# Moving the mixer's first product in front of a couple's scores in a fused attention and MLP kernel

## The chip, the cores and the metric

The kernel runs on one core of a Trainium2 chip. The time is the device time of one execution in microseconds (us). Of the kernel before, three timed runs gave 573.91, 575.65 and 576.12 us, so the median is 575.65 us. One more execution was taken with the hardware profiler: its own time is 570.46 us, and the span from its first to its last instruction is 568.7 us.

The core has five engines with a queue each: TensorE (PE, the matrix products; its weight loads are shown apart as PEld), VectorE (DVE), ScalarE (ACT), GpSimd (POOL) and SyncE (SP, which here only issues DMAs). Each engine works through its own queue in order. An instruction that needs another engine's result waits on a semaphore, and everything behind it in its queue waits with it.

## The reference

The reference is attention with normalised queries and keys, and then a mixing layer and an MLP on its output. There are 8 batches, 12 heads, 448 tokens and 64 values per head:

```python
q_n, k_n = rmsnorm(q, g_q), rmsnorm(k, g_k)
scores = q_n @ k_n.transpose(0, 1, 3, 2) / sqrt(64)
attn = softmax(scores)
x = (attn @ v).transpose(0, 2, 1, 3).reshape(8, 448, 768)
h = x.transpose(0, 2, 1) @ U @ V            # U: 448 x 32, V: 32 x 448, over the tokens
u = x + h.transpose(0, 2, 1)
out = u + relu(u @ w_ch1) @ w_ch2           # 768 -> 3072 -> 768
```

## The kernel before

The heads are worked on in groups of four, three groups to a batch, numbered gi = 0 to 23. A group has two couples of two heads, written (batch, pr) with pr = 0 to 5; couple (2, 0) is the first of group 6.

**Staging of a group.** Queries and keys are loaded (`load`, issued by SP), squared and summed (`squares`, `sums`), and scaled by their root mean squares (`scale_all`; from group 6 on by POOL, lines 198 and 202). From group 6 on the turning of queries and keys, so that the 64 head dimensions lie on the partitions, is done by DMA: `turn_dma` (lines 388 to 394) issues four DMA transposes on SP's queue, in the order qT of the first couple, kT of the first, qT of the second, kT of the second. Then `take_dma` (line 399) multiplies each couple's qT by the gains on POOL, in place. A couple's scores need that product and the couple's kT.

**A couple's scores.** `Spair` (line 445) makes one couple's scores. Two products go into two small PSUM tiles `sl` (line 455, 64 rows of the array, 448 columns), four into two large tiles `sc` (line 464), and one last block, whose keys are the remaining 64 of both heads together, into a third small tile (`Slast`, lines 473 to 480, product at line 476). Each is followed by its exponential on ACT (lines 457, 468, 477). For a couple that comes with the remaining rows of the group before (`rest`), the last block is a step of its own; for the others it is issued inside `Spair` (line 466).

**Values.** `Vall` (line 551) multiplies the exponentials by the values and divides by the sums (DVE, lines 545 and 546). `Rest` (line 597) does the last 64 rows of a group of four heads (PE line 568, DVE lines 580 and 584, output `xr`).

**The mixer and the MLP of a batch.** `mix_t` (line 604) is the mixer's first product: 16 narrow products with U (line 609, 32 columns of the array each, 12 on `x` and 4 on `xr`), copied to `tT` by DVE (line 613). `mix_two` (line 617) is the second: products with V into two `sc` tiles (line 626), four additions on DVE (line 633), and DMA transposes of the result into `uT` (line 639, SP). `up` (line 689) is the first MLP product, 1.14 by the planner's cost, with a ReLU on ACT. `down` (line 733) is a quarter of a second MLP product: six products of 384 columns (line 740), cost 0.98; after the fourth quarter DVE adds the residual (line 750) and SP issues the output's DMAs (line 758).

PSUM is a pool `ps` of four small tiles (for `sl`, `po`, `pu`, `ph`, `pv`, `pr`) and a pool `ps_sc` of two large ones (for the `sc` tiles of scores and of `mix_two`).

**What sets the order.** After a front written out by hand, a loop at the end of the function (lines 1051 to 1089) merges two lists as the program is built. `att` holds the attention's steps, `mlp` the pieces of mixer and MLP, each in its own order. `done_at` says how far `att` must be before a batch's pieces may run. `due` says how much attention work should have been issued for the MLP work issued so far; a step of `att` is taken if it is due and `ready` says that the engines' planned clocks (`at`, advanced by `runs`) allow it. Two conditions of `ready` matter here: a couple's scores aren't taken directly behind a piece of the mixer, and not where ACT or DVE are planned to be behind PE. Neither the landing of a DMA nor POOL's work is in `at`.

Of the kernel before, what the change touches and what calls it, by code (L numbers as in the profile page):

```python
# [21 lines left out]
REST = 8.0  # L22
SECOND = 53.0
APART = 3


@with_exitstack
def kernel(
# [322 lines left out]
    at = {"pe": 0.0, "act": 0.0, "dve": 0.0}  # L351
    exp_done = {}

    def runs(eng, us):
        at[eng] = us + (at["pe"] if eng == "pe" else max(at["pe"], at[eng]))
# [86 lines left out]
        runs("act", 0.9 if n == 2 else 0.52)  # L442
        exp_done[(b, pr)] = at["act"]

    def Spair(b, pr, rest=None):
        qT, kT = qk[divmod(b * NPAIR + pr, 2)]
        E = es[(b, pr)] = ep.tile([P, NB, S], BF16, name="E", tag="E")
        ts = [ps.tile([P, 512], FP32, name="sl", tag="ps")[:, :S] for _ in range(2)]
        if rest is not None:
            rest_tile(rest)  # L450
            rest_products(rest)
            rest_norms(rest)
        for i in range(2):
            d = slice(i * D, (i + 1) * D)
            nc.tensor.matmul(ts[i], kT[d, 2 * P:3 * P], qT[d], start=True, stop=True)  # L455
        for i in range(2):
            nc.scalar.activation(E[:, 4 + i, :], ts[i], AF.Exp, scale=scal, bias=bias)  # L457
        runs("pe", 0.4)
        runs("act", 1.04)
        tiles = [ps_sc.tile([P, 2, 512], FP32, name="sc", tag="sc") for _ in range(2)]  # L460
        for r in range(2):
            for i in range(2):
                d = slice(i * D, (i + 1) * D)
                nc.tensor.matmul(tiles[r][:, i, :S], kT[d, r * P:(r + 1) * P], qT[d], start=True, stop=True)  # L464
        if rest is None:
            Slast(b, pr)
        for r in range(2):
            nc.scalar.activation(E[:, 2 * r:2 * r + 2, :], tiles[r][:, :, :S], AF.Exp, scale=scal, bias=bias)  # L468
        runs("pe", 0.4)
        runs("act", 1.78)  # L470
        exp_done[(b, pr)] = at["act"]

    def Slast(b, pr):
        qT, kT = qk[divmod(b * NPAIR + pr, 2)]
        last = ps.tile([P, 512], FP32, name="sl", tag="ps")[:, :S]
        nc.tensor.matmul(last, kT[:, SM:], qT, start=True, stop=True)  # L476
        nc.scalar.activation(es[(b, pr)][:, 2 * NJ, :], last, AF.Exp, scale=scal, bias=bias)  # L477
        runs("pe", 0.2)
        runs("act", 0.52)
        exp_done[(b, pr)] = at["act"]  # L480
# [78 lines left out]
    def rest_products(gi):  # L559
        b = groups[gi][0]  # L560
        va, vl = normed[gi][2:]
        pv = rest_tiles[gi]
        q0 = 0 if b % 2 else SM
        for lp in range(2):
            E = es[divmod(2 * gi + lp, NPAIR)]
            for j in (NJ, *range(NJ)):
                for e in range(2):
                    nc.tensor.matmul(  # L568
                        pv[e * R:(e + 1) * R, lp, :],
                        E[:, 2 * j + (e if j < NJ else 0), q0:q0 + R],  # L570
                        va[:, (lp + 2 * e) * NJ + j, :] if j < NJ else vl[:, lp, e * D1:(e + 1) * D1],
                        start=(j == NJ), stop=(j == NJ - 1))
        runs("pe", 0.36)

    def rest_norms(gi):
        b, h0, _ = groups[gi]
        pv = rest_tiles.pop(gi)
        lo, hi = (0, R) if b % 2 else (R, P)
        r = headp.tile([P, 2], FP32, name="r", tag="r")
        nc.vector.reciprocal(r, pv[:, :, D])  # L580
        for e in range(2):
            rows = slice(e * R, (e + 1) * R)
            c = (h0 + 2 * e) * D
            nc.vector.tensor_tensor(
                x_rest[b % 2][lo:hi, c:c + 2 * D].rearrange("p (h d) -> p h d", d=D),
                pv[rows, :, :D],
                r[rows].rearrange("p h -> p h ()").to_broadcast([R, 2, D]), ALU.mult)
        runs("dve", 0.6)
# [5 lines left out]
    def rest_tile(gi):  # L594
        rest_tiles[gi] = ps.tile([P, 2, D1], FP32, name="pr", tag="ps")
# [166 lines left out]
    att = []  # L762

    def add_att(cost, f, *a):
        att.append((cost, f, a))
# [3 lines left out]
    def weights(n):  # L769
        for f, a in todo[:n]:  # L770
            f(*a)
        del todo[:n]
# [8 lines left out]
    for i, (b, pr) in enumerate(pairs):  # L781
        if b == 0:
            continue
        gi, a = divmod(i, 2)
# [3 lines left out]

        rest = gi - 1 if a == 0 and (pr > 0 or b > APART) else None
        if a == 0 and pr == 0 and b > 1:  # L790
            add_att(0.8, Vall, *pairs[i - 1])
            if gi == DMA_FROM:
                add_att(0.0, sums, gi + 1, 0)
                add_att(0.0, sums, gi + 1, 1)
                add_att(0.0, scale_all, gi + 1)
            if b <= APART:
                add_att(0.5, Rest, gi - 1)
# [63 lines left out]
    done_at = {0: 0}  # L861
# [7 lines left out]
    mlp = []  # L869
# [135 lines left out]
    ia = im = 0  # L1005
    ca = cm = 0.0
# [12 lines left out]
    def due(c):  # L1019

        if c < m_one:
            return min(a_one - 0.01, a_one * c / (m_one - 3.0))
        c -= m_one
        if c < REST:
            return a_one - 0.01
        if c < SECOND:
            return a_one + (a_two - a_one) * (c - REST) / (SECOND - REST)
        return a_two + (a_all - a_two) * (c - SECOND) / (m_end - m_one - SECOND)

    def mixes(f):  # L1030
        return f in (mix_t, mix_two)

    def ready(f, a):
        if f is Spair:
            if im > 0 and mixes(mlp[im - 1][1]):
                return False
            return at["dve"] <= at["pe"] + 0.3 and at["act"] <= at["pe"] + 0.6
        if f is Slast:
            return not after_pair
        if f in (Vall, Rest) and ca >= a_one and (after_pair or after_v):  # L1040
            return False
        if f is sums and a[0] > DMA_FROM:
            return not any(m[1] is mix_t for m in mlp[max(0, im - 1):im + 3])
        if ca >= a_one:
            return True
        if f is Vall:
            return exp_done[a[:2]] <= at["pe"] + 0.1
        return f is not Srows or at["act"] <= at["pe"] + 0.6 and (len(a) == 1 or a[1] is None or at["dve"] <= at["pe"] + 0.9)

    later, turning, mixed, after_pair, after_v = [], False, False, False, False  # L1050
    while ia < len(att) or im < len(mlp):
        if not turning:
            held = []
            for f, a in later:
                if a[0] == DMA_FROM + 2 and not mixed:
                    held.append((f, a))
                else:
                    f(*a)
            later[:] = held
        may_mlp = im < len(mlp) and ia >= done_at[mlp[im][3]]  # L1060
        take_att = ia < len(att) and (not may_mlp or ca <= due(cm) and ready(*att[ia][1:]))
        if take_att:
            c, f, a = att[ia]
            if f is load:
                later.append((f, a))
            else:
                f(*a)
            after_pair = after_pair or f is Spair
            after_v = after_v or f is Vall
            if ia >= a_from:  # L1070
                ca += c
            ia += 1
            if f is scale_all and a[0] < DMA_FROM:
                weights(2)
            if f is T and a == (DMA_FROM - 1, 1):
                nc.vector.memset(kp[:, 2 * NJ:], 0.0)
        else:
            f = mlp[im][1]
            if after_pair and mixes(f) or f is mix_two and max(at["act"], at["dve"]) > at["pe"]:
                e = next((i for i in range(im, len(mlp)) if mlp[i][1] is down), None)  # L1080
                if e is not None and mlp[e][3] < mlp[im][3]:
                    mlp.insert(im, mlp.pop(e))
            after_pair = after_v = False
            c, f, a, _ = mlp[im]
            f(*a)
            turning = f is mix_t or turning and not (f is mix_two and a[1][1] == NW - 1)
            cm += c
            mixed = mixed or f is mix_two and a[1][1] == NW - 1
            im += 1
# [30 lines left out]
```

## Time and profile before

| | |
|---|---|
| median of three timed runs | 575.65 us |
| the profiled execution's own time | 570.46 us |
| its span | 568.7 us |
| PE busy | 561.5 us, 99% of the span |
| ACT busy | 308.5 us, 54% |
| POOL busy | 204.5 us, 36% |
| DVE busy | 189.4 us, 33% |
| products of line 693 (`up`) | 223.9 us, 352 ns each |
| products of line 740 (`down`) | 223.5 us, 326 ns each |

In rows of the profile's timeline the first number is the start in us from the span's start and the second how long the group lasts; then engine, line, operation, output<-inputs, shapes, and the count of merged instructions. In brackets stands how long the engine was idle before and what ended that. A matmul's own duration is longer than the distance to the next one, because products overlap in the array. SPq rows are SP's DMA issues, not the transfers.

### The profile page before, as it was taken

The page shows a single profiled execution, that of the slowest core. Times are in us where ns is not written, and L with a number is a line of the kernel's source. Part 1 is how long each engine was busy: PE and PEld are TensorE (multiplying, and loading weights), DVE is VectorE, ACT ScalarE, POOL GpSimd, SP SyncE. Part 2 cuts the span into 40 slices and gives each one's busy share as a digit, 9 for nine tenths or more (in the row PEclk, how much of TensorE's full clock was granted, in tenths as well). Part 3 has the DMA queues.
Part 4 walks back from the last instruction along what each step waited for, and adds up shares of the span by engine and source line. Part 5 has one row for each costly group of instructions (what it writes and reads, how often), then busy time and mean ns, then how long its engine had stood idle before and what let it go on. Part 6 is the DMA issues. An engine that isn't in the chain of part 4 may idle for free.

```text
span 568.7 us, 11567 instructions
## 1 busy us (share of the span) xinstructions
PE 561.5 (99%) x4756; PEld 321.9 (57%) x4756; DVE 189.4 (33%) x425; ACT 308.5 (54%) x518; POOL 204.5 (36%) x308
## 2 busy tenths in 40 slices
PE   8899999999999999999999999999999999999997
PEld 7665555555555555555556555565465555555555
DVE  6955564312443222521235231532034210410011
ACT  6967760888454776287553677367752544014300
POOL 6874784355332724343522532351531000000000
PEclk9999999999999999999999999999999999999999
DMA  9999999784247633595335735375215200320022
GB/s 241 223 242 240 247 228 179 159 225 114 62 91 171 170 98 63 90 233 144 74 96 107 203 90 125 67 204 128 36 33 86 56 23 0 77 56 0 1 57 56
DMA packets 104830, 68.20 MB, mean 120 GB/s; under 512 B 66633, under 2 KB 100937, under 8 KB 104777
## 3 DMA queue, kind: packets, MB, share of 16 engines
q1 hardware_dynamic: 95124, 57.83, 44.2%
q0 software_dynamic: 9408, 9.44, 10.0%
q8 instruction: 37, 0.61, 0.5%
q10 hardware_dynamic: 244, 0.20, 0.1%
q14 instruction: 17, 0.13, 0.1%
HBM read 52.20 MB, written 11.01 MB: 111 GB/s over the span
## 4 chain that ended last, share of the span: by engine, by line
PE 94%; ACT 4%; DMA 1%; DVE 0%; POOL 0%; issue 0%; POOLq 0%
PE po L740 38%; PE ph L693 37%; PE pv L541 4%; ACT E L435 3%; PE sc L464 2%; PE sl L455 2%; PE sl L476 2%; PE pr L568 1%; PE po L727 1%; PE pv L537 1%; PE sc L430 1%; PE sc L711 1%; PE sc L626 1%; PE pu L609 1%; DMA ob<-in_g_k_dram 1%; PE pt L368 1%
## 5 line engine op out<-in xcount | busy, mean ns | idle before, releaser
L693 PE MATMUL ph<-uT,w1b 128*128 128x448 bf16 x1128 | 223.9, 352 | 0.0
L740 PE MATMUL po<-w2b,hT 128*128 128x384 bf16 x1296 | 223.5, 326 | 0.0
L740 PEld LDWEIGHTS <-hT 128*128 128x128 bf16 x1296 | 122.8, 98 | 84.1 <-issue 7.0
L693 PEld LDWEIGHTS <-w1b 128*128 128x128 bf16 x1128 | 108.2, 98 | 97.6 <-issue 2.2
L700 ACT ACTIVATE hT<-ph 128x448 bf16<-128x448 f32 x187 | 99.7, 550 | 106.9 <-PE ph L693 106.5
L399 POOL TENSOR_SCALAR qT<-qT,gg 128x448 bf16<-128x448 bf16 x36 | 50.4, 1402 | 92.4 <-DMA qT<-qn 77.3
L457 ACT ACTIVATE E<-sl,gg 128x448 bf16<-128x448 f32 x72 | 41.6, 630 | 76.2 <-PE sl L455 75.3
L198 POOL TENSOR_TENSOR qn<-qf,rs 128x384 bf16<-128x384 f32 x36 | 29.9, 830 | 111.9 <-ACT rs L175 106.1
L468 ACT ACTIVATE E<-sc,gg 128x896 bf16<-128x896 f32 x72 | 68.9, 1019 | 0.0
L750 DVE TENSOR_TENSOR ob<-po,x 128x384 f32<-128x384 f32 x46 | 25.6, 557 | 103.7 <-PE po L740 103.0
L167 DVE TENSOR_REDUCE ssq<-sq 128x14 f32<-128x896 f32 x45 | 47.0, 1078 | 23.9 <-ACT sq L141 23.2
L545 DVE RECIPROCAL r<-pv 128x6 f32<-128x6 f32 x42 | 8.2, 195 | 125.4 <-PE pv L541 125.1
L435 ACT ACTIVATE E<-sc,gg 128x896 bf16<-128x896 f32 (+1 forms) x42 | 37.0, 951 | 1.1 <-PE sc L430 0.7
L541 PE MATMUL pv<-va,E 128*128 128x65 bf16 x756 | 35.4, 194 | 0.0
L541 PEld LDWEIGHTS <-E 128*128 128x128 bf16 x756 | 32.4, 98 | 3.2
L198 POOL TENSOR_TENSOR kp<-kf,rs 128x384 bf16<-128x384 f32 x36 | 29.8, 828 | 0.0
L537 PE MATMUL pv<-vl,E 128*128 128x130 bf16 x126 | 27.6, 219 | 0.0
L633 DVE TENSOR_TENSOR x<-sc,x 128x384 bf16<-128x384 f32 x42 | 20.8, 550 | 17.4 <-PE sc L626 17.4
L546 DVE TENSOR_TENSOR x<-pv,r 128x384 bf16<-128x384 f32 x42 | 23.4, 557 | 1.4
L174 ACT ACTIVATE rs<-ssq,eps 128x28 f32<-128x28 f32 x20 | 6.3, 315 | 32.1 <-DVE ssq L167 32.1
L477 ACT ACTIVATE E<-sl,gg 128x448 bf16<-128x448 f32 x36 | 23.3, 646 | 0.0
L206 POOL CAST va<-vf 128x768 bf16<-128x768 f32 x24 | 20.7, 862 | 0.2 <-DMA vf<-in_v_dram 0.2
(130 smaller groups left out, 426.4 us busy)
## 6 DMA issues: line engine op xcount, KB each, us to landing
qf<-in_q_dram SPq DMA_DIRECT2D x23, 448.0 KB, 3.7
kf<-in_k_dram SPq DMA_DIRECT2D x23, 448.0 KB, 4.9
vf<-in_v_dram SPq DMA_DIRECT2D x48, 192.0 KB, 5.5
out_dram<-ob SPq DMA_DIRECT2D x48, 192.0 KB, 2.7
w2b<-in_moe_w_ch_dram POOLq DMA_DIRECT2D x8, 576.0 KB, 15.3
w1b<-in_moe_w_ch_dram POOLq DMA_DIRECT2D x2, 1152.0 KB, 17.6
vf<-in_v_dram SPq DMA_DIRECT2D x48, 32.0 KB, 5.1
w1b<-in_moe_w_ch_dram POOLq DMA_DIRECT2D x1, 1536.0 KB, 28.5
```

Of the source, the lines that this page charges most:

```text
L167: nc.vector.tensor_reduce(ssqs[gi][:, i, :], sqs.pop((gi, i)), AX, ALU.add)
L198: nc.gpsimd.tensor_tensor(main.rearrange("p (t i) d -> p i t d", i=2), src[:, c, :2 * NJ].rearrange("p (i t) d -> p i t d", i=2), rs[:, c, ...
L399: nc.gpsimd.tensor_scalar(qT[:, a], qT[:, a], gg[:, 0:1], None, ALU.mult)
L435: nc.scalar.activation(es[(b, pr)][:, 2 * r:2 * r + n, :], sc[:, :n, :S], AF.Exp, scale=scal, bias=bias)
L457: nc.scalar.activation(E[:, 4 + i, :], ts[i], AF.Exp, scale=scal, bias=bias)
L468: nc.scalar.activation(E[:, 2 * r:2 * r + 2, :], tiles[r][:, :, :S], AF.Exp, scale=scal, bias=bias)
L537: nc.tensor.matmul(pv[:, i].rearrange("p e d -> p (e d)"), E[:, 2 * NJ, w:w + P], vl[:, lp, :], start=True, stop=False)
L541: nc.tensor.matmul(pv[:, i, e, :], E[:, 2 * j + e, w:w + P], va[:, (lp + 2 * e) * NJ + j, :], start=False, stop=(e == 1 and j == NJ - 1))
L693: nc.tensor.matmul(ph, w1b[:, dt, ht * P:(ht + 1) * P], uT[:, dt, off:off + S], start=(dt == 0), stop=(dt == KD - 1))
L700: nc.scalar.activation(hT[:, ht, off:off + S], ph, AF.Relu)
L740: nc.tensor.matmul(po, hT[:, ht, col:col + P], w2b[:, ht, half * HALF:(half + 1) * HALF], start=(ht == 0), stop=(ht == KH - 1))
L750: nc.vector.tensor_tensor(ob[:, h], po, urows(b, col, half), ALU.add)
```

## The change

In the merging loop, ahead of the usual choice, the planner looks whether `mix_t` is among the next four pieces of `mlp` (`NEAR`), and whether the next step of `att` is a `Spair` without `rest` that is due within 1.0 (`AHEAD_OF`), with ACT's and DVE's planned clocks not behind PE's. If so, it issues `mix_t` at once, directly behind it the couple's `Spair` without its last block, and puts the last block (`Slast`) into `att` as the next step, which may be taken after one more piece of MLP.

```diff
+NEAR, AHEAD_OF = 4, 1.0
...
-    def Spair(b, pr, rest=None):
+    def Spair(b, pr, rest=None, late=False):
...
-        if rest is None:
+        if rest is None and not late:
             Slast(b, pr)
...
+        near = next((m for m in range(im, min(im + NEAR, len(mlp))) if mlp[m][1] is mix_t), None)
+        if near is not None and ia >= done_at[mlp[near][3]] and ia < len(att) and not after_pair and not after_v:
+            c, f, a = att[ia]
+            if f is Spair and a[2] is None and ca <= due(cm) + AHEAD_OF and at["act"] <= at["pe"] + 0.6 and at["dve"] <= at["pe"] + 0.3:
+                m = mlp.pop(near)
+                m[1](*m[2])
+                cm += m[0]
+                turning = True
+                f(*a, True)
+                att.insert(ia + 1, (0.0, Slast, a[:2]))
+                for d in done_at:
+                    if done_at[d] > ia:
+                        done_at[d] += 1
+                after_pair = True
+                ca += c
+                ia += 1
+                continue
         may_mlp = im < len(mlp) and ia >= done_at[mlp[im][3]]
```

In the program that is built, this holds at two places. The order of the queues of SP and POOL stays as it was; PE's, ACT's and DVE's differ at these places alone.

First place (couple (2, 0), mixer of batch 1; n down stands for n pieces of `down`):

```text
before: mix_t(1), 3 down, mix_two, 4 down, mix_two, 2 down, Spair(2,0)+Slast, 2 down, turn_dma(7), 1 down, Spair(2,1), 1 down, Vall(2,0)
after:  mix_t(1), Spair(2,0), 3 down, mix_two, 4 down, mix_two, 4 down, Slast(2,0), turn_dma(7), Spair(2,1), 2 down, Vall(2,0)
```

Second place (couple (3, 0), mixer of batch 2):

```text
before: Rest(8), 2 down, Spair(3,0)+Slast, 1 down, mix_t(2), 2 down, mix_two, 1 down, turn_dma(10)
after:  Rest(8), 1 down, mix_t(2), Spair(3,0), 4 down, mix_two, 1 down, Slast(3,0), turn_dma(10)
```

## The prediction

> **What bounds the kernel now.** I read the page first: the busy shares and the chain that ended last.
>
> ```profile
> span 568.7 us, 11567 instructions
> PE 561.5 (99%) x4756; PEld 321.9 (57%) x4756; DVE 189.4 (33%) x425; ACT 308.5 (54%) x518; POOL 204.5 (36%) x308
> ...
> PE 94%; ACT 4%; DMA 1%; DVE 0%; POOL 0%; issue 0%; POOLq 0%
> ```
>
> PE is busy for 99% of the span and carries 94% of the chain. So there are no gaps of PE to fill: a reordering of the same products can gain only what PE loses between unlike products, and any wait that it gives PE is paid in full, since nothing later on PE has idle time into which the delay could vanish. The question is whether the moved products find their inputs ready. I therefore went through the timeline of the first place, from the issue of group 6's DMA transposes to couple (2, 1):
>
> ```profile
> 82.36 1.33 SPq L391 DMA_TRANSPOSE qT<-qn  x1
> 84.22 1.21 SPq L393 DMA_TRANSPOSE kT<-kp  x1
> ...
> 88.17 0.43 PE L609 MATMUL pu<-x,Ub 128*32 128x192 bf16 x12
> ...
> 88.62 3.10 PE L740 MATMUL po<-w2b,hT 128*128 128x384 bf16 x18
> ...
> 91.65 0.34 PE L626 MATMUL sc<-tT,Vr 32*128 32x192 bf16 x8
> ...
> 92.42 1.41 POOL L399 TENSOR_SCALAR qT<-qT,gg 128x448 bf16<-128x448 bf16 x1 [8.45 <-DMA qT<-qn]
> ...
> 94.11 1.40 POOL L399 TENSOR_SCALAR qT<-qT,gg 128x448 bf16<-128x448 bf16 x1 [0.28 <-DMA qT<-qn]
> ...
> 98.27 0.36 PE L455 MATMUL sl<-qT,kT 64*128 64x448 bf16 x2
> ...
> 98.66 1.16 ACT L457 ACTIVATE E<-sl,gg 128x448 bf16<-128x448 f32 x2 [12.36 <-PE sl L455]
> ...
> 98.94 0.36 PE L476 MATMUL sl<-qT,kT 128*128 128x448 bf16 x1
> ...
> 99.14 3.09 PE L740 MATMUL po<-w2b,hT 128*128 128x384 bf16 x18
> ...
> 99.71 0.64 ACT L477 ACTIVATE E<-sl,gg 128x448 bf16<-128x448 f32 x1
> ...
> 100.23 1.92 ACT L468 ACTIVATE E<-sc,gg 128x896 bf16<-128x896 f32 x2
> ```
>
> `mix_t(1)` starts at 88.17, its last product is followed by `down` at 88.62, and couple (2, 0)'s scores begin at 98.27, nearly 10 us later. Between the two POOL multiplies the couple's qT by the gains: it had been idle for 8.45 us until the transpose landed, starts at 92.42 and ends at 93.83. The second row of line 399 is couple (2, 1)'s. In the kernel before the scores come 4.4 us after that product, so its lateness costs nothing. Why it is late is seen in the DMA view of the stretch 82.3 to 88.5, and in the view by tile of qT:
>
> ```profile
> q0 software_dynamic: 1301, 0.98, 103.8%
> ...
> qT<-qn SPq DMA_TRANSPOSE x2, 8.5
> kT<-kp SPq DMA_TRANSPOSE x2, 9.3
> ```
>
> ```profile
> DMA to landing us min/median/max: 2.5/2.5/8.5
> ```
>
> The transposes share the DMA engines with the software queue, on which POOL's issues of w2 are still running; here a transpose takes 8.5 to 9.3 us to land, against 2.5 us in the median of the whole span. kT of the couple, issued at 84.22, lands at about 84.22 + 9.3 = 93.5.
>
> **The change, part by part.** No product, exponential, addition or DMA is added or removed. Two `Spair` go earlier and two last blocks later; neither they nor `mix_t` issue a DMA or anything on POOL, so SP's and POOL's queues keep their order.
>
> First place, the score products. After the change they stand directly behind `mix_t`, so PE reaches them at 88.62, where `down` began before. They need qT, multiplied at 92.42 + 1.41 = 93.83, and kT at 93.5. From a product's end to ACT's start it is 0.03 us here (98.27 + 0.36 against 98.66); with as much for POOL to PE, the scores start at 93.86 and PE waits 93.86 - 88.62 = 5.2 us. Nothing covers this: PE's queue is in order, and the three `down` that stood there wait behind the scores, with them the additions of line 750, the output's DMAs, `mix_two` and, on SP, the transposes into `uT`, all about as much later. Lower bound of the wait: were the first qT to land after 8.5 us, like the one of that row, POOL would end at 82.36 + 8.5 + 1.41 = 92.3, which leaves 3.7 us. Upper bound: were the second multiplication needed too, 94.11 + 1.40 - 88.62 = 6.9 us. I take 5.2, since the built program has the first score product wait for the first multiplication alone.
>
> First place, changes of the kind of product. A `down` quarter is six products; 18 of them take 99.14 to 102.16, where the next scores begin, and 12 take 96.21 to 98.27:
>
> ```profile
> 96.21 2.12 PE L740 MATMUL po<-w2b,hT 128*128 128x384 bf16 x12
> ...
> 102.16 0.36 PE L455 MATMUL sl<-qT,kT 64*128 64x448 bf16 x2
> ```
>
> With two lengths the pace and the loss at the change come out: (3.02 - 2.06) / 6 = 0.16 us a product, and 2.06 - 12 x 0.16 = 0.14, about 0.1 us. Entering or leaving a narrow product costs that. `mix_t` directly in front of the scores saves one such change, and the last block fills the whole array like `down` and costs none beside it: 0.1 us saved at each place, 0.2 in all.
>
> First place, the last block. It now stands directly in front of couple (2, 1)'s scores. That couple's own last block reuses the small PSUM tile that the exponential of line 477 frees. From the rows, a last block's exponential is done 0.39 + 0.64 = 1.03 us after its product starts, and couple (2, 1)'s last block comes 0.20 (98.94 to 99.14) + 0.67 (98.27 to 98.94) + 0.1 = 0.97 us after it: a wait of 0.1 us, between 0 and 0.6 if ACT has something else to end. ACT's order otherwise only lets the two large exponentials go ahead of the last block's. `mix_two` now takes the large PSUM tiles from those: they are done 0.39 + 1.05 (98.66 to 99.71) + 1.92 = 3.4 us after the scores start, and PE needs 0.67 + 0.1 + 18 x 0.16 = 3.7 us to get there. No wait, but if ACT were over 0.3 us late there would be one.
>
> Second place. Here `mix_t(2)` goes ahead of one `down` less behind `Rest(8)`:
>
> ```profile
> 138.04 1.40 POOL L399 TENSOR_SCALAR qT<-qT,gg 128x448 bf16<-128x448 bf16 x1 [1.16 <-DMA qT<-qn]
> ...
> 150.51 2.12 PE L740 MATMUL po<-w2b,hT 128*128 128x384 bf16 x12
> ...
> 150.83 0.59 DVE L584 TENSOR_TENSOR xr<-pr,r 64x128 bf16<-64x128 f32 x2
> ...
> 152.57 0.36 PE L455 MATMUL sl<-qT,kT 64*128 64x448 bf16 x2
> ```
>
> qT is multiplied by 139.4, some 12 us ahead. `mix_t` would start at 150.51 + 6 x 0.16 + 0.1 = 151.6 and needs `xr` for its last products; DVE ends it at 150.83 + 0.59 = 151.42. So nothing is paid, at most 0.2 us if DVE slips; ACT has four `down` for its exponentials, one more than at the first place. That leaves the 0.1 us saved.
>
> PE's clock. A PE idle for 5.2 us may come back at half its rate. This trace shows both sides of it, in the timeline's first row and in stretches (length, then busy time and count by engine, then the granted clock):
>
> ```profile
> 1.36 5.73 PE L245 MATMUL busy<-ident 128*128 128x128 bf16 x72 [1.36 <-POOL ident masks.py:199]
> ```
>
> ```profile
> 0.00:4.60 4.60, 3.24 (x31) 3.25 (x32) 1.04 (x13) 1.53 (x2) 0.86 (x7) 1.00 0.59 184
> ...
> 565.30:567.80 2.50, 0.00 (x0) 0.00 (x0) 0.28 (x1) 0.00 (x0) 0.00 (x0) 1.00 0.30 79
> 567.80:568.70 0.90, 0.00 (x0) 0.00 (x0) 0.00 (x0) 0.00 (x0) 0.00 (x0) 0.51 0.00 0
> ```
>
> At the start, 31 products take 3.24 us, 105 ns each, and the other 41 of the 72 end at 7.09, some 60 ns each: PE begins at about half rate for 3.2 us of work, which costs 31 x 45 ns = 1.4 us. At the end, 2.5 us without a product are followed by a granted clock of 0.51. So I expect a 5.2 us wait to lower the clock, and I price the return like the start: 1.4 us, with ends of 0 (the clock stays) and 3.2 (two such stretches at half rate, 6.5 us of which half is lost).
>
> The Trainium skill, "TensorE: Matmul & The Clock Gate", Part 1, says that the clock halves after an idle window of about 3.4 us, that these windows run freely, and that a busy window restores it. By that, a 5.2 us wait would hold a whole window in (5.2 - 3.4) / 3.4, about half of all phases, and the sum would lack the 1.4 us in the other half. The end of this trace, where 2.5 us sufficed, speaks for the clock to fall more often than that.
>
> **The sum.** 5.2 + 0.1 - 0.2 + 1.4 = 6.5 us. Against the profiled execution that is 570.46 + 6.5 = 577.0 us, and a span of 575.2. The timed runs lie higher, with their median at 575.65; I put the 6.5 us on it: 582.2 us.
>
> **The rivals.**
>
> The wait without the loss of clock: 5.2 + 0.1 - 0.2 = 5.1 us, so 580.8 us. For it: no stretch inside this span shows PE idle for so long, so the fall is inferred from its two ends. Against it: the row at 567.80.
>
> The wait is hidden (the other side). If the software queue has drained a few us earlier in timed runs than in the profiled one, the transposes land after the usual 2.5 us: qT at 84.9, multiplied by 86.3, kT at 86.7, all before PE's 88.62. Then only the saved changes remain: 575.65 - 0.1 = 575.5 us, no measurable difference. It decides at a landing of qT by 88.62 - 1.41 = 87.2, 5.2 us earlier than in this trace; and kT too must land by 88.6 instead of 93.5. Against it: the queue's 103.8% and landings of 8.5 and 9.3 us, which no part of the change touches.
>
> The change pays by more than the 0.2 us: no row shows PE time that it could recover, with PE busy for 99% of the span; it would take 2.9 us.
>
> **How the numbers follow.** This kernel's measurement tells apart about 0.5%, 2.9 us. Wait with loss of clock 0.62, wait alone 0.26, hidden 0.10, a gain 0.02. Both waits are slower by more than 0.5%: slower 0.88, same 0.10, faster 0.02. The low end is the shortest wait without loss of clock, 575.65 + 3.7 - 0.2 = 579.2, less 0.7 for the scatter of the runs: 578.5. The high end is 5.2 + 0.6 - 0.2 + 3.2 = 8.8, so 584.5, and 0.5 for the scatter: 585.
>
> **What would show it.** In the changed profile, a single gap on PE of about 5 us in front of the first products of line 455, at 88.6, ended by POOL's qT of line 399; behind it products of line 740 at twice their pace's time for some 3 us and a granted clock under 1; everything later by 5 to 7 us; at the second place no wait. I am wrong if those products start before 91 us, if qT's landing has moved, or if PE has new gaps elsewhere.

## The result, and the profile after

The changed kernel took 579.86 us (median of six runs, 579.10 to 582.61) against 574.83 us for the kernel before in the same session (572.50 to 576.12). The ratio is estimated at 1.0119, with a 95% interval of 1.0090 to 1.0148: slower, by more than the 0.5% that this measurement tells apart. The plain quotient of the two medians is smaller, 1.0088, just below that interval; the stretches and the second measurement below show which of the two is nearer. The profiled execution took 582.61 us, with a span of 580.8 us.

From the changed kernel's page: the span, the busy times, the granted clock in 40 slices (tenths) and the chain that ended last.

```profile
span 580.8 us, 11566 instructions
...
PE 566.2 (97%) x4756; PEld 324.2 (56%) x4756; DVE 189.9 (33%) x425; ACT 309.4 (53%) x518; POOL 204.5 (35%) x308
...
PEclk9799998999999999999999999999999999999999
...
PE 87%; DMA 4%; POOL 4%; ACT 2%; issue 2%; DVE 0%; SPq 0%; POOLq 0%
```

The products are as many as before (4756). PE's share of the chain fell from 94 to 87%, and DMA and POOL now hold 4% each. The granted clock (PEclk) has two dips, in the second slice and in the seventh (87 to 102 us).

The timeline of SP, PE and POOL at the first place, after the change. Line numbers of the code below the change are one higher than before: `Rest` is line 569, `mix_t` 610, a couple's first scores 456, `down` 741, POOL's gain on qT 400.

```profile
87.51 1.34 SPq L392 DMA_TRANSPOSE qT<-qn  x1
...
89.92 0.22 PE L569 MATMUL pr<-vl,E 128*64 128x65 bf16 x2
...
93.33 0.43 PE L610 MATMUL pu<-x,Ub 128*32 128x192 bf16 x12
...
96.83 1.41 POOL L400 TENSOR_SCALAR qT<-qT,gg 128x448 bf16<-128x448 bf16 x1 [7.71 <-DMA qT<-qn]
...
98.29 0.56 PE L456 MATMUL sl<-qT,kT 64*128 64x448 bf16 x2 [4.45 <-POOL qT L400]
98.63 0.97 PE L465 MATMUL sc<-qT,kT 64*128 64x448 bf16 x4
99.53 5.09 PE L741 MATMUL po<-w2b,hT 128*128 128x384 bf16 x18
104.55 0.34 PE L627 MATMUL sc<-tT,Vr 32*128 32x192 bf16 x8
```

PE is idle for 4.45 us in front of the scores, and the multiplication of qT ends that. kT is hardly sooner: the load of it as PE's weights waits for its transpose until 98.28. Then the 18 products of the next three `down` take 99.53 to 104.55, 5.02 us, where they took 3.03 us before (88.62 to 91.65). The same stretch in windows (length, then busy time and count by engine, PE first, then the granted clock, the DMA share and GB/s):

```profile
93.60:96.79 3.19, 0.24 (x12) 0.01 (x4) 0.36 (x1) 0.00 (x0) 0.00 (x0) 1.00 1.41 134
96.79:98.29 1.50, 0.00 (x0) 0.01 (x1) 0.00 (x0) 0.00 (x0) 1.41 (x1) 0.50 1.39 149
98.29:103.61 5.32, 5.32 (x19) 2.24 (x20) 0.02 (x1) 2.96 (x4) 5.10 (x8) 0.50 0.09 31
103.61:107.00 3.39, 3.39 (x28) 1.85 (x27) 2.48 (x5) 0.00 (x0) 1.75 (x5) 1.00 0.25 61
```

The clock falls to half during the wait and stays there for 5.3 us of work behind it: 19 products in 5.32 us, then, at the full clock, 28 in 3.39 us.

**Where the 12 us between the two profiled spans come from.** Three starts, each of a `Rest`, cut the span into parts that hold the same work in both kernels. In the kernel before:

```profile
84.77 0.22 PE L568 MATMUL pr<-vl,E 128*64 128x65 bf16 x2
...
150.14 0.22 PE L568 MATMUL pr<-vl,E 128*64 128x65 bf16 x2
...
167.87 0.22 PE L568 MATMUL pr<-vl,E 128*64 128x65 bf16 x2
```

and after, beside the row at 89.92:

```profile
162.36 0.22 PE L569 MATMUL pr<-vl,E 128*64 128x65 bf16 x2
...
179.99 0.22 PE L569 MATMUL pr<-vl,E 128*64 128x65 bf16 x2
```

| part | before, us | after, us | difference |
|---|---|---|---|
| start to Rest(5), ahead of any changed instruction | 84.8 | 89.9 | +5.1 |
| Rest(5) to Rest(8), with the first place | 65.4 | 72.4 | +7.1 |
| Rest(8) to the next, with the second place | 17.73 | 17.63 | -0.1 |
| from there to the end | 400.8 | 400.8 | 0.0 |

The first part isn't the change's: the instructions up to there are the same. In this execution PE waited in the front for data and its clock fell there too:

```profile
22.12 0.55 PE L431 MATMUL sc<-qT,kT 64*128 64x448 bf16 x2 [2.47 <-DVE kT L384]
```

```profile
21.69:28.52 6.83, 6.00 (x53) 3.78 (x54) 5.82 (x22) 4.63 (x8) 5.32 (x9) 0.50 0.85 155
```

The wait and half of these 6.0 us of work make 5.5 us, about the difference. The front varies so in both kernels: of the eleven profiles in the table below, three start Rest(5) after 88 us, one of them with the order of the kernel before, and each of the three has a clock of one half for 6.83 us in the front; the other eight start it at 84.7 to 86.0 us and have no such dip. From Rest(5) to the end, which leaves it out, the kernel before takes 568.7 - 84.8 = 483.9 us and the changed one 580.8 - 89.9 = 490.9 us: +7.0 us, or 1.2% of the span. I use this stretch for the experiments.

### The profile page after: what moved, and what is told of

Its sections match the earlier page's. It is cut to its first block, busy times and chain, and to the rows that moved or that the text cites. A ratio compares the mean times of both kernels' runs of the same rounds, so it can differ in the third digit from the quotient of the medians.

```text
span 580.8 us, 11566 instructions
## 1 busy us (share of the span) xinstructions
PE 566.2 (97%) x4756; PEld 324.2 (56%) x4756; DVE 189.9 (33%) x425; ACT 309.4 (53%) x518; POOL 204.5 (35%) x308
## 4 chain that ended last, share of the span: by engine, by line
PE 87%; DMA 4%; POOL 4%; ACT 2%; issue 2%; DVE 0%; SPq 0%; POOLq 0%
PE po L741 36%; PE ph L694 35%; PE pv L542 4%; DMA kf<-in_k_dram 3%; PE sc L465 2%; PE sl L456 2%; DMA qT<-qn 2%; PE sl L477 2%; ACT E L436 1%; POOL sq L145 1%; PE po L728 1%; PE pr L569 1%; PE pv L538 1%; PE sc L712 1%; PE sc L627 1%
```

## The experiments

My theory: all of the loss is at the first place, as a wait for group 6's operands and as work at half clock behind it; the second place gains a tenth of a microsecond. The rivals are in the expectations: that the moves themselves cost something, that the slow products have another cause than the wait, that the operands are late for another reason than the loads of w2.

| kernel | Rest(5) starts | span | Rest(5) to end | PE's wait in front of couple (2, 0) | median | ratio to before, 95% interval |
|---|---|---|---|---|---|---|
| before | 84.77 | 568.7 | 483.9 | - | | |
| changed | 89.92 | 580.8 | 490.9 | 4.45 | 579.86 | 1.0119 (1.0090 to 1.0148) |
| changed, again | 88.79 | 580.2 | 491.4 | 5.12 | 579.30 | 1.0119 (1.0084 to 1.0154) |
| second place only | 84.90 | 568.7 | 483.8 | - | 571.90 | 1.0002 (0.9985 to 1.0018) |
| first place only | 85.06 | 577.0 | 491.9 | 5.62 | 578.47 | 1.0110 (1.0086 to 1.0134) |
| wait filled | 84.69 | 574.0 | 489.3 | 1.33 beside the filling | 576.00 | 1.0076 (1.0058 to 1.0094) |
| last block inside | 85.69 | 575.7 | 490.0 | 4.69 | 578.84 | 1.0129 (1.0104 to 1.0155) |
| no last w2 | 84.91 | 568.7 | 483.8 | none | 571.27 | 1.0000 (0.9980 to 1.0019) |
| before, no last w2 | 88.57 | 572.8 | 484.2 | - | 571.43 | 1.0006 (0.9991 to 1.0021) |
| pair two later | 85.95 | 575.2 | 489.3 | 3.03 | 577.91 | 1.0114 (1.0089 to 1.0139) |
| pair four later | 85.00 | 574.2 | 489.2 | 1.39 | 576.16 | 1.0088 (1.0055 to 1.0122) |

The starts, spans and waits come from each kernel's profile, the fourth column is span less start. The ratios are to runs of the kernel before taken beside them.

**Which place it is.** The trigger was limited to one couple:

```diff
-            if f is Spair and a[2] is None and ca <= ...
+            if f is Spair and a[2] is None and a[:2] != (2, 0) and ca <= ...   # second place only
+            if f is Spair and a[2] is None and a[:2] == (2, 0) and ca <= ...   # first place only
```

> The change at the second place alone (mixer of batch 2 with couple (3, 0)). The stretch from the first product of Rest(5) to the end of the span is free of the front's scatter: 483.9 us before, 490.9 after. Theory (all of the loss is the wait and the lowered clock of the first place; the second saves one change of the kind of product): 483.8 us, and a time within 0.5% of before. Rival (the moves themselves, an earlier mixer product and a late last block, cost something wherever they are made): over 485 us.

> The change at the first place alone (mixer of batch 1 with couple (2, 0)). Theory: the whole loss, a stretch from Rest(5) to the end of about 491.0 us (490.9 of the changed kernel and the 0.1 that the second place saved), some 1.0 to 1.2% slower than before, with a PE wait of 4 to 5.5 us that POOL's multiplication of qT ends. Rival (the loss is shared by both places): at most 488 us.

The second place alone: 483.8 us, no measurable difference in time. The first alone: 491.9 us, 1.1% slower; the changed kernel's loss is all there. Its trace holds something that I had not put first:

```profile
88.47 0.43 PE L610 MATMUL pu<-x,Ub 128*32 128x192 bf16 x12
88.73 0.26 PE L610 MATMUL pu<-xr,Ub 128*32 128x192 bf16 x4
...
91.80 1.41 POOL L400 TENSOR_SCALAR qT<-qT,gg 128x448 bf16<-128x448 bf16 x1 [7.53 <-DMA qT<-qn]
...
94.61 0.55 PE L456 MATMUL sl<-qT,kT 64*128 64x448 bf16 x2 [5.62 <-DMA kT<-kp]
```

Here qT was ready at 93.2, and PE waited on for kT's transpose until 94.6. So two operands are late by about as much, and which one ends the wait differs between executions: POOL's qT in both profiles of the changed kernel, the transpose of kT in this one, in "wait filled", "last block inside" and both of the later pairs. A faster multiplication alone would have gained next to nothing: where POOL ended the wait, PE's load of kT had itself waited for the transpose, until 98.28 us with the scores at 98.29 in the changed kernel, and until 97.55 with the scores at 97.84 in "changed, again". The scores' rows of "changed, again" and "last block inside":

```profile
97.84 0.56 PE L456 MATMUL sl<-qT,kT 64*128 64x448 bf16 x2 [5.12 <-POOL qT L400]
```

```profile
94.31 0.56 PE L456 MATMUL sl<-qT,kT 64*128 64x448 bf16 x2 [4.69 <-DMA kT<-kp]
```

**Whether the clock is a loss of its own.** The wait was filled with products that change no result:

```diff
-NEAR, AHEAD_OF = 4, 1.0
+NEAR, AHEAD_OF, FILL = 4, 1.0, 72
...
+        if late and (b, pr) == (2, 0):
+            for _ in range(FILL):
+                nc.tensor.matmul(ts[0][:, :P], ident, ident, start=True, stop=True)
         for i in range(2):
             d = slice(i * D, (i + 1) * D)
             nc.tensor.matmul(ts[i], kT[d, 2 * P:3 * P], qT[d], start=True, stop=True)
```

> The changed kernel with 72 products of identity by identity (128 columns, 56 ns apart, 4.0 us) in front of couple (2, 0)'s first score product, into a PSUM tile that the scores then overwrite: additional work that changes no result. The wait for qT stays, but PE is busy through most of it. Theory (the wait lowers PE's clock and that is a second loss of some 2.4 us): clock stays at full speed, products of line down at 163 ns after the scores, stretch from Rest(5) to the end about 488.5 us. Rival (the slow products after the wait have another cause, or cost nothing): about 491 us.

Its timeline and windows (the additional lines make the scores line 459 and `down` line 744; the filling is line 456):

```profile
88.10 0.43 PE L613 MATMUL pu<-x,Ub 128*32 128x192 bf16 x12
...
88.55 4.19 PE L456 MATMUL sl<-ident 128*128 128x128 bf16 x72
...
94.08 0.36 PE L459 MATMUL sl<-qT,kT 64*128 64x448 bf16 x2 [1.33 <-DMA kT<-kp]
...
94.75 3.10 PE L744 MATMUL po<-w2b,hT 128*128 128x384 bf16 x18
```

```profile
92.60:94.08 1.48, 0.14 (x4) 0.01 (x2) 0.00 (x0) 0.00 (x0) 0.00 (x0) 1.00 1.41 97
94.08:97.50 3.42, 3.42 (x23) 1.88 (x24) 0.56 (x1) 2.96 (x4) 3.16 (x4) 1.00 0.17 59
```

The scores still start 5.53 us after PE could have begun them (88.55 to 94.08), yet the clock stays at 1.00 and the 18 products take 3.10 us instead of 5.09. The stretch is 489.3 us, 5.4 over before: the wait, within 0.1 us, and nothing else. "First place only" lost 8.0 us, 2.6 more. Of these 0.16 are a longer wait (scores 6.14 us after the start of `mix_t` there, 88.47 to 94.61, and 5.98 here, 88.10 to 94.08) and 0.1 the second place's gain, which it lacks; so 2.3 us is what the half clock cost there. Additional, useless work made the kernel faster than the one with the same wait unfilled. That the stretch isn't at the expected 488.5 is the longer wait of this execution (5.98 us from the start of `mix_t` to the scores, against 4.96 in the changed kernel, 93.33 to 98.29).

**The late last block.** `Slast` was put back into `Spair` at both places:

```diff
-                f(*a, True)
-                att.insert(ia + 1, (0.0, Slast, a[:2]))
-                ...
+                f(*a)
```

> The changed kernel, but with the last score block inside Spair again at both places, as before. Theory: the late last block is worth one change of the kind of product, about 0.1 us a place, and costs couple (2, 1) a wait of about 0.1 us at the first place, so the stretch from Rest(5) to the end is 490.9 to 491.2 us. Rival (the late last block holds up couple (2, 1) or its values): under 490.5 us.

490.0 us is below the 490.9 to 491.2 expected, which is a miss, and its ratio is no better than the changed kernel's. The stretch alone would have pointed to the rival; the windows show where the 0.9 us are:

```profile
94.13:97.54 3.41, 3.23 (x13) 1.23 (x14) 0.00 (x0) 2.56 (x4) 2.83 (x4) 0.50 0.29 75
97.54:101.00 3.46, 3.46 (x29) 1.88 (x28) 1.45 (x3) 1.03 (x2) 3.46 (x8) 1.00 0.11 26
```

PE works at half clock for 3.2 us here, against 5.3 in the changed kernel: about 1.0 us less lost, with a wait 0.24 us longer. That leaves nothing that could be put down to the block's place within 0.2 us. The block's own price is read better where nothing waits, in "no last w2" below.

**Why the operands are late.** The last two loads of w2, 1.15 MB that POOL issues shortly before the transposes, were left out, in the changed kernel and in the kernel before; the products that would use that quarter of w2 use another quarter of it, so a part of the output is computed with other weights:

```diff
-... for half in range(2) for c in range(4)]
+... for half in range(2) for c in range(4)][:-2]
...
-w2b[:, ht, half * HALF:(half + 1) * HALF],
+w2b[:, ht - 12 * (half == 1 and ht >= 12), half * HALF:(half + 1) * HALF],
```

> The changed kernel without the last two loads of w2 (1.15 of its 4.6 MB in bfloat16, issued by POOL shortly before the transposes of group 6); the products that would use that quarter of w2 use another quarter that is loaded, so the second half of the MLP's output is computed with other weights. All products stay. Theory (the transposes are late because of the software queue's w2 traffic): the first qT lands some 2.5 to 4 us after its issue instead of 8.5, PE does not wait or waits under 1 us, and the stretch from Rest(5) to the end is that of the kernel before without these loads, less 0.2 us. Rival (the transposes are late for another reason, such as their own queue): PE waits 4 us or more, and the stretch stays near 491 us.

> The kernel before without the same two loads of w2, computing with another quarter of it in their place: what the missing loads alone do. Both theories: a stretch from Rest(5) to the end of 483.9 us, since PE did not wait there before; the front may be faster by some us, as it shares the DMA engines.

The DMA view of the stretch 82.2 to 89.3 of the changed kernel without these loads, and its timeline:

```profile
q0 software_dynamic: 304, 0.22, 20.3%
...
qT<-qn SPq DMA_TRANSPOSE x2, 2.5
kT<-kp SPq DMA_TRANSPOSE x2, 2.7
```

```profile
86.00 1.41 POOL L400 TENSOR_SCALAR qT<-qT,gg 128x448 bf16<-128x448 bf16 x1 [1.87 <-DMA qT<-qn]
...
88.58 0.26 PE L610 MATMUL pu<-xr,Ub 128*32 128x192 bf16 x4
...
88.77 0.36 PE L456 MATMUL sl<-qT,kT 64*128 64x448 bf16 x2
```

The software queue's share is 20.3%, against 102.9% in the kernel before and 105.9% in "first place only" over the same stretch; the transposes land in 2.5 and 2.7 us (8.5 and 9.3 before, 9.5 and 10.1 in "first place only"), and the scores follow `mix_t` without a wait. The stretch is 483.8 us, 0.1 less than before. That the missing loads do not shorten it by themselves is seen in the kernel before without them: 484.2 us, 0.3 more than with them. From Rest(5) to Rest(8) it takes as long as the kernel before, 65.37 us (84.91 to 150.28): at the first place the change of product saved and the last block's wait cancel. The lateness is the loads'. This also measures the rival of a hidden wait: with landings of 2.5 us no time is lost.

**Later by pieces.** In the changed kernel the three mixer pieces of batch 1 go two or four MLP pieces later, and the trigger is changed so that the couple still comes directly behind `mix_t`:

```diff
+    LATER = ...                       # 2 or 4
+    for part in (("two", (2, 3)), ("two", (0, 1)), ("t", None)):
+        j = ...                       # this piece of batch 1's mixer in mlp
+        mlp.insert(j + LATER, mlp.pop(j))
...
-        if near is not None and ia >= ...
+        if near is not None and (mlp[near][3] > 1 or near == im) and ia >= ...
...
-            if f is Spair and a[2] is None and ca <= ...
+            if f is Spair and a[2] is None and (a[:2] == (2, 0) or ca <= ...    # LATER = 2 alone
```

> The changed kernel with the mixer's three pieces of batch 1, and the couple with them, two MLP pieces (2.0 us) later. Theory (a wait for qT that lasts until POOL is done, paid one for one): wait 4.5 - 2.0 = 2.5 us, up to 3.2; the clock falls if 2.5 us without a product are enough, as at the end of the span, or stays. Stretch from Rest(5) to the end 483.9 + 2.5 - 0.2 = 486.2 us with the clock kept, up to 489 with it lowered. Rival (the wait is not for something that comes by a clock of its own, but is made by the order): near 491 us.

> The same with four MLP pieces (3.9 us). Theory: wait 0.6 us, up to 1.3, no fall of the clock, stretch from Rest(5) to the end 484.3 to 485.0 us. Rival: near 491 us.

The wait shrinks to 3.03 and 1.39 us, the first within what was expected (2.5, up to 3.2), the second just over it (0.6, up to 1.3). The stretches miss the expected 486.2 to 489 and 484.3 to 485.0: they are 489.3 and 489.2 us. I had left out SP's queue. The mixer's transposes into `uT` stand on it ahead of `turn_dma(7)`, so the next group's transposes come later, and couple (2, 2) is what waits next. SP's last transpose into `uT` and the first of `turn_dma(7)` in the kernel before:

```profile
98.97 1.21 SPq L639 DMA_TRANSPOSE uT<-u_rest  x1
...
105.45 1.24 SPq L391 DMA_TRANSPOSE qT<-qn  x1
```

From the timeline of "pair four later":

```profile
105.08 1.21 SPq L640 DMA_TRANSPOSE uT<-u_rest  x1
...
110.28 1.24 SPq L392 DMA_TRANSPOSE qT<-qn  x1
...
114.30 2.81 POOL L400 TENSOR_SCALAR qT<-qT,gg 128x448 bf16<-128x448 bf16 x2 [11.33 <-DMA qT<-qn]
...
115.76 0.37 PE L456 MATMUL sl<-qT,kT 64*128 64x448 bf16 x2 [1.99 <-POOL qT L400]
```

Both are issued later, by 6.1 and 4.8 us, while PE reaches couple (2, 2) only 1.9 us later than before (113.77 against 111.86). The same kernel's windows:

```profile
112.00:116.88 4.88, 2.89 (x33) 1.41 (x32) 1.83 (x4) 3.57 (x9) 2.57 (x2) 1.00 0.90 114
116.88:120.29 3.41, 3.41 (x11) 1.40 (x10) 0.00 (x0) 3.17 (x5) 3.41 (x8) 0.50 0.92 281
```

It is 1.39 + 1.99 us of waiting and 3.41 us at half clock, 1.7 lost: 5.1 of the 5.3 us over before. With two pieces it is 3.03 and 0.91, and some 1.5 at half clock (0.54 granted over 3.15 us). So a wait was moved rather than removed, and these two kernels answer the question about the wait, but offer no better order.

**A second measurement.**

> The changed kernel once more, beside the kernel before on the same chip, for a narrower interval. Theory (loss at the first place alone, wait plus lowered clock): stretch from Rest(5) to the end 490 to 492 us against 483.9, ratio 1.011 to 1.014. Rival (the difference of the first medians, 5.0 us, is all there is): ratio under 1.010.

579.30 us against 572.79, ratio 1.0119 again, stretch 491.4. The 5.0 us between the first two medians is the low side of this, since the kernel before took 574.83 us there, against 571.3 to 572.8 beside the experiments; whether its front was the reason isn't shown. The rival named in the expectation is not out by the times alone, whose interval reaches down to 1.0084; what speaks against it are the stretches, 7.0 and 7.5 us over before. No version beats both kernels: the second place alone, the change's gain without its loss, can't be told from the kernel before.

## Why the prediction was right

The forecast of 582.2 us, +6.5, has the sign, the place and the mechanism; the measured 579.86 us is inside its range, and the stretch says +7.0. That the two sizes agree so well is partly luck: two terms were off by 0.7 and 1.2 us in opposite directions. By its steps:

- **PE's 99%: a wait is paid in full.** Right. Behind the second place the two kernels take the same 400.8 us.
- **The wait, 5.2 us within 3.7 to 6.9.** Measured 4.45, 5.12, 5.62 and 4.69 us in the four profiles with the pair at its place and the wait unfilled. The changed kernel's is shorter than forecast because the transpose came sooner: POOL could start on qT 9.3 us after its issue (87.51 to 96.83), against 10.1 us before (82.36 to 92.42). That qT's multiplication ends it was right for the changed kernel; that kT, put at 0.3 us less, could be the later one was not weighed, and it is in half of these profiles.
- **Its cause, the software queue's loads.** Shown by leaving two of them out. The rival of a hidden wait is out for this kernel: every profile with the pair at its place shows the wait, and it is absent only in the one without the last loads.
- **PE's clock, 1.4 us.** Right that it falls, wrong in size: 2.6 us in the changed kernel. The 18 products cost 5.02 - 3.03 = 2.0 more, and the six score products 1.24 (98.29 to 99.53) instead of 0.67 (94.08 to 94.75 in "wait filled"), 0.6 more. I priced the return like the start of the span, with 3.2 us of work at half rate; it was 5.3 us of work. My upper end, two stretches, was the nearer. The rival without a fall of the clock is out: it fell in every profile with an unfilled wait of 3 us or more, and the twelve runs of the changed kernel had mean granted clocks of 0.988 to 0.994, against 0.994 to 1.000 for the kernel before (beside the experiments; a fall in the front alone gives 0.994, as in the profile of "before, no last w2") and 0.996 to 1.000 for "wait filled".
- **Changes of the kind of product, 0.1 us a place.** The second place shows it: 17.73 to 17.63 us.
- **The late last block's wait, 0.1 us.** Right: couple (2, 1)'s last block starts 0.59 us after the large score products in the changed kernel (113.50 to 114.09), against 0.47 before (102.36 to 102.83), and the balance of "no last w2" agrees.
- **The second place: no wait.** Right.
- **The sum.** 4.5 + 2.6 + 0.1 - 0.2 = 7.0, as measured in the stretch. The forecast's 6.5 came from a wait put 0.7 too long and a clock put 1.2 too short. The profiled time of 577.0 was missed by 5.6 us, and 5.1 of these lie in the front, ahead of the change.

The Trainium skill, "TensorE: Matmul & The Clock Gate", Part 1, would have had the clock fall in about half of the phases of a 5.2 us wait (an estimate from its figure), since it asks for a whole idle window of about 3.4 us. These runs differ: it fell for waits of 3.03, 4.45, 4.69, 5.12 and 5.62 us, and after shorter ones (below); in the changed kernel it fell 2.95 us after the wait began (93.84 to 96.79). The lengths for which it stayed low here, 3.41 us and twice that, agree with the Trainium skill's window, and so does its rule that a busy window restores the clock: in the changed kernel PE was busy throughout the last 3.41 us ahead of the return at 103.61.

## What to carry to other kernels

Before a step is moved ahead, look in the timeline at when each of its operands was ready, those that come by DMA and by an engine off the critical path above all: a planner that counts only some engines will put the step where its operands aren't, and on an engine that is busy for 99% of the span all of that wait is lost. A DMA's usual time to landing says little while a bulk load shares the engines (8.5 us here against 2.5). A wait of a few us on TensorE also costs work at half clock behind it, here about half as much again as the wait itself (2.6 us beside 4.45, 2.3 beside 5.62).

## What the runs showed that I had not expected

- The clock fell after far shorter waits than that of the change: after 1.99 us in "pair four later", and then only 1.1 us behind the wait's end (115.76 to 116.88), and in the fronts after 2.47 us (changed), 1.82 ("changed, again") and 1.58 us ("before, no last w2", a wait that ends at 20.46 and a clock of one half from 20.82). It did not fall after 1.33 us (in the filled kernel), nor after 1.39 ("pair four later").
- In these runs it stays at half for one or two steps of 3.41 us: one where PE had work for almost all of the first step (3.23 of 3.41 us in "last block inside"), two where the wait reached well into it (the changed kernel from 96.79 to 103.61, 6.8 us, with work from 98.29). So the price of a wait depends on where it ends, by about 1 us: 3.2 or 5.3 us of work at half rate.
- Seventy-two useless products in a wait made the kernel faster by some 2 us than the same order without them.
